# Selecting a chunk's blocks behind its ranks, a fetch at a late hand-out, a later gate for logits, and W1 halves in two even runs

## The chip, the cores and the metric

One core of one Trainium2 chip. The metric is the device time of one execution in microseconds (us): the median of three runs. A profiled execution beside them gives the time of every instruction. The engines: TensorE (PE, its weight loads PEld), VectorE (DVE), ScalarE (ACT), GpSimd (POOL) and the queue of SyncE (SP), which issues most of the transfers.

## The reference

A causal mixing step over seven tokens, then a mixture of experts with one expert a token:

```
x = conv(x, softmax(weight))           # 8 sequences x 3584 tokens x 192, 8 groups of 24 columns
logits = norm(x) @ norm(expert_emb).T / tau          # 28672 tokens, 8 experts
e = argmax(logits);  g = softmax(logits)[e]
out = g * (relu(x @ w1[e]) @ w2[e])    # w1[e]: 192 x 1024, w2[e]: 1024 x 192
```

## The kernel before

**Stages.** The tokens are cut into 16 chunks of 1792 (16 tiles of 112). For a chunk, `mix` computes the convolution on TensorE and the norms; `route` scales the rows, makes a two-part half-precision form of them, transposes it, computes the logits on TensorE, ranks each token within its expert, and leaves 16 scatters pending. Each scatter (POOL, line 959) writes 112 rows into a DRAM area sorted by expert, `rows_d`. Once 16 more scatters have been issued, and if the next chunk's number is in `PICK` (3, 4, 5, 6, 8, 10, 12, 14), `put` marks it and `settle` hands out new blocks: `hand_out` calls `pick`, which works out how many whole blocks of 1024, 512 or 256 tokens must exist whatever the routing was, and `select` computes on DVE, in 21 small instructions (17 without the update of the start positions), which expert and which first row each of them has. A block's expert is known only on the chip: SP and DVE load it from the tile `sel` into a register.

**A block.** `expert` works on up to 512 tokens. `fetch` issues on SP a transposing transfer of the block's rows from `rows_d` (line 1087) and of its gates and token numbers (line 1090), and names the scatters that it needs. DVE copies the expert's W1 (line 1069) and W2 (line 1072) into one `slot`. TensorE computes the hidden layer (`h_ps`, line 1142), ACT takes the relu as the first half-precision part (line 1146), DVE the rest as the second (line 1148), TensorE computes the output (`o_ps`, line 1170), ACT scales it and POOL sends it out (line 1177). Blocks are up to three ahead in fetching.

**W1 halves.** Behind a block of 128 tokens the next W1 is copied in two halves, each as soon as the hidden layer has done with the old half; behind other blocks in one piece. The last blocks (22 of 128 tokens among 512s and 256s) make most of the halves: 48 copies of a half in all.

**Order.** SP's queue keeps the order in which the program issues. The order on the other engines is arranged by the framework, under hints: `under` puts an instruction behind the last hidden part on DVE, `over` behind the last ACT step, `behind` behind the last matmul. The program is written by one Python loop in `run`: it writes the blocks' work, and between two pieces of a block as much work of `mix` and `route` as fits. These are generators: each yields how many us of DVE and ACT work it has written, and is continued when the slack of the block's pieces, times a rate, has paid for it (`steer` sets the rate from `COST`, the DVE and ACT work of a chunk). A yielded `_Gate` holds a generator until the planner's clock `clk` has passed a time: the logits of a group (4 tiles) wait for the time at which SP has issued the group's transposes plus `LAND_T`.

**The transposes on SP.** For chunks 3 to 15, `route` has a group's four row transposes done by SP (line 955). There are two buffers: the sets of groups 0 and 1 are written as their rows are ready, the sets of groups 2 and 3 right behind the logits of groups 0 and 1. After each group's logits the loads of parts of a later chunk's x (line 480) are written. A fetch is written at the start of a block, so a set of transposes stands before or behind it on SP by the planner's clock.

Of the kernel before, what the change touches and what calls it, by code (L numbers as in the profile page):

```python
# [17 lines left out]
ALU = mybir.AluOpType  # L18
# [12 lines left out]
NT = 16  # L31
CT = TP * NT
# [9 lines left out]
PICK = (2, 3, 4, 5, 6, 8, 10, 12, 14)  # L42
GX = 4
NACT = 3
OUT = 1.9, 1.6
COST = 17.4, 15.6
WAIT = 0.5, 0.5
COST_A, COST_B = 10.0, 26.5
LEAD = 16.0
# [2 lines left out]
KMAX = 32  # L52
MORE = 3
# [8 lines left out]
LATE = 1.0  # L62
PICKED = 5.0
ACTS = 8, 10, 16
LAND_X, LAND_T = 9.0, 4.5
TURN, FETCH, PIECE = 5.1, 2.1, 1.4
RANK_L, RANK_P = 2.0, 1.5
STEP1, STEP2, STEPC, STEPL = 1.08, 1.98, 0.65, 0.62
SPACE, EVICT, SAVED = 1.54, 0.6, 8.0
SIGNAL, MOVED = 0.15, 1.8  # L70
DONE = 2.6, 7.9
# [67 lines left out]
class _Moe:  # L139
    def __init__(self, ctx, tc, x, weight, emb, tau, w1, w2, out):  # L140
        self.tc, self.nc = tc, tc.nc
        self.x, self.weight, self.emb, self.tau = x, weight, emb, tau
        self.w1, self.w2, self.out = w1, w2, out
        B, S, _ = x.shape
        self.B, self.S, self.N = B, S, B * S
        self.nch = self.N // CT
        self.per_b = S // CT
        self.cap = self.N + PAD
        self.dummy = E * self.cap
        pool = lambda name, bufs, **k: ctx.enter_context(  # L150
            tc.tile_pool(name=name, bufs=bufs, **k))
        self.cp = pool("const", 1)
        self.xp = pool("xload", 2)
        self.xtp = pool("xtrans", 2)
        self.sp = pool("small", 2)
        self.lp = pool("lone", 1)
        self.ep = pool("expert", 3)
        self.fp = pool("flip", 2)
        self.yp = pool("y", 3)
        self.op = pool("out", 4)  # L160
        self.mp = pool("meta", 6)
        self.rings = {k: pool("ps_" + k, n, space=PSUM)
                      for k, n in (("r", 2), ("l", 1), ("h", 5))}

        self.res1 = self.cp.tile([128, E * IMG], F16, name="res1")
        self.res2 = self.cp.tile([128, E * IMG], F16, name="res2")
        self.slot = self.cp.tile([128, RES], F16, name="slot")
        self.rows = [self.cp.tile([TP, NT, RW], I32, name=f"rows{k}")
                     for k in range(2)]
        self.hid = self.cp.tile([128, 2 * NFC * 512], F16, name="hid")  # L170
        self.dp = pool("scratch", 1, space=DRAM)
        self.rows_d = self.dp.tile([E * self.cap + PAD, RW], I32, name="rows_d")
        self.scatters, self.pend, self.step = [], [], None
        self.drop = self.cp.tile([128, D], F16, name="drop")
        self.acc = self.cp.tile([128, 2 * E], F32, name="acc")
        self.counts, self.pace = {}, 1.0
        self.due_out, self.sent_at, self.next_out = 0.0, 0.0, None
        self.whole = None
        self.xts, self.mixed = [], {}
        self.clk, self.gated, self.mm = 0.0, False, None  # L180
        self.asked, self.sp_at, self.low, self.parts = {}, 0.0, None, []
        self.need = 0
        self.subs, self.ready, self.flips, self.at, self.copied = [], 0, 0, 0, 0


# [609 lines left out]
    def route(self, c):  # L795
        xTs = []
        nc, sp = self.nc, self.sp
        xc, s, si, f = self.mixed.pop(c)
        r32 = self.rows[c % 2]
        rows = r32[:].bitcast(F16)  # L800
        for g in range(0, NT, GX):
            u = slice(g, g + GX)
            sb = s[:, u].unsqueeze(2).to_broadcast([TP, GX, D])
            self.under(nc.vector.tensor_tensor(  # L804
                out=xc[:, u, :], in0=xc[:, u, :], in1=sb, op=ALU.mult).ins)
# [3 lines left out]
                out=rows[:, u, 256:384], in0=xc[:, u, 0:128],  # L809
                in1=rows[:, u, 0:128], op=ALU.subtract).ins)  # L810
            self.under(nc.vector.tensor_tensor(
                out=rows[:, u, 192:256], in0=xc[:, u, 128:192],
                in1=rows[:, u, 128:192], op=ALU.subtract).ins)
# [7 lines left out]
        for g in range(NT // GX):  # L821
            if c > DIRECT:
                if len(xTs) == g:
                    xTs.append((self.turn(rows, g * GX, GX), self.queue(TURN)))
                xT, at = xTs[g]
                yield _Gate(at + LAND_T)
            else:
                xT = self.xtp.tile([128, GX, 3, TP], F16, tag="xT", name="xT")
                for k in range(3):
                    tp = self.ps("r", [128, GX, TP], F16, "tr_ps")  # L830
                    for a in range(GX):
                        self.behind(nc.tensor.transpose(
                            out=tp[:, a, :],
                            in_=rows[:, g * GX + a, k * 128:(k + 1) * 128],
# [4 lines left out]
            for a in range(GX):  # L839
                for k in range(3):  # L840
                    i = nc.tensor.matmul(  # L841
                        out=lg[:, g * GX + a, :], lhsT=xT[:, a, k, :],
# [12 lines left out]
        if self.gated and self.step is not None:  # L855
# [4 lines left out]
            out=l, in_=lg.rearrange("p t (k e) -> p t e k", k=2), op=ALU.add,  # L860
# [14 lines left out]
                                op=ALU.mult)  # L875
        nc.vector.scalar_tensor_tensor(
            out=l, in0=l, scalar=0.0, op0=ALU.is_equal,
            in1=self.e8[:].unsqueeze(1).to_broadcast([TP, NT, E]), op1=ALU.mult)
# [4 lines left out]
                                op=ALU.is_equal)  # L883
# [5 lines left out]
            out=fl(inc[:]), data0=fl(self.rst[:]), data1=fl(oh[:]), initial=0.0,  # L889
# [12 lines left out]
            out=off, in0=pc[:TP, 0, :], in1=self.cb[:TP, :], op=ALU.add).ins)  # L902
        nc.vector.tensor_tensor(out=self.cb, in0=pc[:, 1, :], in1=self.cb,
                                op=ALU.add)
# [10 lines left out]
            out=di, in_=dr, scalar=-1.0, op=ALU.add)  # L915
        yield 0.8, 0.0
        self.pend += [(c, di[:, t:t + 1], r32[:, t, :]) for t in range(NT)]
        if c == self.nch - 1:
            self.pads()


    def put(self, step=None):
        if not self.pend:
            return
        c, idx, src = self.pend.pop(0)
        self.scatter(idx, src)
        if step is not None:
            _dep(self.tc, self.scatters[-1], step.name)
        if c < self.nch and len(self.scatters) % NT == 0:
            self.left += CT  # L930
            if c + 1 in PICK[1:]:
                self.whole = c + 1


    def settle(self):
        if self.whole is not None:
            self.hand_out(self.whole)
            self.whole = None


    def tick(self, us, i):
# [43 lines left out]
        self.pend += [(self.nch, p[:, e:e + 1], z) for e in range(E + 1)]  # L985


    def select(self, n, k, last, name, cb):
        nc, cp = self.nc, self.cp
        sh = n.bit_length() - 1  # L990
        one = lambda nm, shape=(1, E), dt=F32: self.lp.tile(
            list(shape), dt, tag="sl_" + nm, name="sl_" + nm)
        av, ai = one("av"), one("ai", dt=I32)
        nc.vector.tensor_tensor(out=av, in0=cb, in1=self.start,
                                op=ALU.subtract)
        nc.vector.tensor_single_scalar(out=ai, in_=av,
                                       scalar=float(n - 1 if last else 0),
                                       op=ALU.add)
# [45 lines left out]
                op0=ALU.mult, op1=ALU.add)  # L1044
        for j in range(k):
            for u in range(0, n, 512):
                self.subs.append((sel, j, n, u, self.need))


    def copy_w1(self, at, halves=(0, 1)):  # L1050
        nc = self.nc
        if at == len(self.subs) or self.subs[at][3]:
            return
        halves = [h for h in halves if self.copied <= 2 * at + h]
        if not halves:
            return
        if halves[0] == 0:
            sel, j = self.subs[at][:2]
            (i,), (self.we,) = nc.values_load_multi_w_load_instructions(
                sel[0:1, j, 0:1], engines=[nc.vector.engine], min_val=0,  # L1060
                max_val=(E - 1) * IMG,
                skip_runtime_bounds_check_because="select clamps it")
            self.under(i.ins)
        self.copied = 2 * at + halves[-1] + 1
        v = self.res1[:, bass.ds(self.we, W2)].rearrange(
            "p (k h f) -> p h k f", k=3, h=2)
        o = self.slot[:, 0:W2].rearrange("p (h k f) -> p h k f", k=3, h=2)
        h = slice(halves[0], halves[-1] + 1)
        self.under(nc.vector.tensor_copy(out=o[:, h], in_=v[:, h]).ins)  # L1069

    def copy_w2(self):
        self.nc.vector.tensor_copy(  # L1072
# [114 lines left out]
            yield OUT  # L1187


    def pick(self, n, last=False, most=KMAX):  # L1190
        k = (self.left + E * (n - 1)) // n if last else max(
            0, -((E * (n - 1) - self.left) // n))
        k = min(k, most)
        at = len(self.subs)
        if k:
            self.select(n, k, last, f"sel{n}_{self.left}", self.now)
            self.left -= k * n
        new = self.subs[at:]
        del self.subs[at:]
        w = max(1, n // 512)  # L1200
        return [new[i:i + w] for i in range(0, len(new), w)]
# [37 lines left out]
    def head(self, first):  # L1239
# [27 lines left out]

        def pick():
            self.left = first * CT
            self.hand_out(first)  # L1270

        def more():
            self.subs += sum(self.pick(128, most=MORE), [])

        n = p = P.add("DVE", 3.8, pick, ranked[-1], pri=PICKED)
        for _ in range(3):
# [6 lines left out]
        self.sp_at = 0.0  # L1283


    def hand_out(self, c):
        self.now, self.need = self.counts[c], NT * c
        for n in (1024, 512, 256) if c < 9 else (1024, 512):
            self.subs += sum(self.pick(n), [])
        self.end = ([p for p in PICK if p > c] + [self.nch])[0]  # L1290


# [14 lines left out]
        self.pace = (due - len(self.scatters)) / max(1.0, steps - MARGIN)  # L1307

    def last_blocks(self):
        self.now, self.need = self.cb[0:1, :], len(self.scatters)  # L1310
        big = self.pick(1024)
        mid = self.pick(512) + self.pick(256)
        small = self.pick(128, True)
        runs = [[((i + o) / (len(g) + o), b) for i, b in enumerate(g)]
                for g, o in ((big, 0.5), (mid, 0.5), (small, 3.0)) if g]
        for _, b in sorted(sum(runs, []), key=lambda v: v[0]):
            self.subs += b
# [69 lines left out]
```

## Time and profile before

| | us |
|---|---|
| median of 3 runs | 1247.41 (1246.84 to 1250.33) |
| the profiled execution | 1254.54 |
| its span, first to last instruction | 1252.8 |
| TensorE busy (matmul) | 1149.4 |
| DVE busy | 898.0 |
| ACT busy | 597.0 |
| POOL busy | 545.9 |

The mean granted clock of TensorE was 0.959 of full speed. Up to about 125 us the experts' weights are loaded and scaled and the first two chunks are routed; up to about 940 us chunks are routed beside the blocks; behind that there are blocks alone. A wait in a row is the idle time of an engine ahead of an instruction, with the instruction whose end released it.

### The profile page before, as it was taken

How to read it: one execution, taken by the hardware profiler on the slowest of the kernel's cores; microseconds unless marked ns; L12 is line 12 of the kernel's file. 1: busy time of each engine (PE TensorE's matmuls, PEld its weight loads, DVE VectorE, ACT ScalarE, POOL GpSimd, SP SyncE). 2: the span in 40 equal slices, each digit the busy share in tenths (PEclk: the TensorE clock that was granted, in tenths of full speed). 3: DMA queues.
4: the chain of work that ended last, by engine and by line, in shares of the span. 5: the costliest groups of instructions: out<-in, count | busy, mean ns of one | idle time of the engine just before them, and what ended most of it. 6: DMA issues, size and time to landing. Idle time of an engine off the chain costs nothing. (4 is left out here: it accounts for less than half of the span.)

```text
span 1252.8 us, 29845 instructions
## 1 busy us (share of the span) xinstructions
PE 1149.4 (92%) x10924; PEld 928.8 (74%) x10924; DVE 898.0 (72%) x2337; ACT 597.0 (48%) x1363; POOL 545.9 (44%) x541
## 2 busy tenths in 40 slices
PE   5637988899899899999899999999999999999997
PEld 3624877787878799678766666776677777889997
DVE  5996979688677878777576766756445566567786
ACT  5777835355253645556353645433433333333332
POOL 1271254564545565454545546455542221222222
PEclk9557999899899999999999999999999999999999
DMA  9851474563636465662736565363222112111211
GB/s 267 249 181 39 94 151 99 125 131 88 143 76 160 90 140 116 139 144 52 155 79 148 113 137 118 70 124 81 67 66 55 46 39 50 49 39 44 46 44 24
DMA packets 269187, 127.79 MB, mean 102 GB/s; under 512 B 210494, under 2 KB 259005, under 8 KB 269040
## 3 DMA queue, kind: packets, MB, share of 16 engines
q1 hardware_dynamic: 245216, 79.00, 29.5%
q0 software_dynamic: 23808, 46.87, 13.8%
q8 instruction: 86, 1.41, 0.5%
q14 instruction: 61, 0.50, 0.1%
q10 hardware_dynamic: 16, 0.01, 0.0%
HBM read 38.35 MB, written 47.53 MB: 69 GB/s over the span
## 5 line engine op out<-in xcount | busy, mean ns | idle before, releaser
L1142 PE MATMUL h_ps<-e_xT,slot 128*128 128x256 f16 (+2 forms) x3232 | 512.5, 291 | 27.8 <-DMA e_xT<-rows_d 18.4
L1170 PE MATMUL o_ps<-slot,hid 128*128 128x192 f16 x5544 | 494.5, 247 | 8.4 <-DVE hid L1148 5.1
L1142 PEld LDWEIGHTS <-slot 128*128 128x128 f16 x4040 | 354.5, 99 | 187.2 <-issue 31.0
L1170 PEld LDWEIGHTS <-hid 128*128 128x128 f16 x5544 | 461.2, 98 | 39.3 <-issue 11.6
L1177 POOL DMA_INDIRECT out_dram<-y,e_mt x231 | 254.3, 1101 | 471.3 <-ACT y L1175 428.4
L1148 DVE SCALAR_TENSOR_TENSOR hid<-h_ps,hid 128x512 f16<-128x512 f32 x462 | 312.7, 686 | 125.5 <-ACT hid L1146 122.9
L1146 ACT ACTIVATE hid<-h_ps 128x512 f16<-128x512 f32 x462 | 272.7, 597 | 233.9 <-PE h_ps L1142 229.0
L959 POOL DMA_INDIRECT rows_d<-rows,di x256 | 274.6, 1073 | 185.6 <-PE h_ps L1142 74.3
L1175 ACT ACTIVATE y<-o_ps,g 128x192 f32<-128x192 f32 x231 | 95.4, 419 | 320.0 <-PE o_ps L1170 294.9
L1142 PE MATMUL h_ps<-e_xf,slot 128*128 128x256 f16 (+2 forms) x808 | 220.4, 289 | 0.6 <-DVE e_xf L1109 0.4
L1072 DVE COPY slot<-res 128x3074 f16 x101 | 99.7, 987 | 139.7 <-PE o_ps L1170 139.1
L1069 DVE COPY slot<-res 128x3072 f16 (+1 forms) x125 | 118.8, 951 | 0.4
L759 PE MATMUL conv_ps<-xt,band 128*112 128x384 f32 x208 | 83.8, 495 | 1.2 <-ACT xt L764 1.2
L1109 DVE COPY e_xf<-e_xT 64x256 f16<-64x256 f16 (+2 forms) x202 | 47.2, 234 | 33.4 <-DMA e_xT<-rows_d 29.3
L764 ACT COPY xt<-conv_ps 112x384 f32<-112x384 f32 x104 | 49.4, 479 | 35.9 <-PE conv_ps L759 32.9
L841 PEld LDWEIGHTS <-xT 128*112 128x112 f16 x672 | 47.5, 132 | 20.9 <-DMA xT<-rows 13.9
L841 PE MATMUL lg_ps<-ma,xT 128*112 128x16 f16 x448 | 49.0, 193 | 11.5 <-DMA xT<-rows 10.8
L771 ACT ACTIVATE sq<-xt 112x192 f32<-112x192 f32 x156 | 55.7, 361 | 3.0 <-DVE sq L775 1.8
L806 ACT CAST rows<-xt 112x768 f16<-112x768 f32 x56 | 45.2, 833 | 16.7 <-DMA rows_d<-rows,di 5.6
L804 DVE TENSOR_TENSOR xt<-xt,x_p_s 112x768 f32<-112x768 f32 x56 | 50.7, 948 | 0.1
L808 DVE TENSOR_TENSOR rows<-xt,rows 112x512 f16<-112x512 f32 x56 | 38.3, 684 | 7.9 <-ACT rows L806 7.0
L841 PE MATMUL lg_ps<-mb,xT 128*112 128x16 f16 x224 | 39.2, 196 | 0.3 <-ACT xT L836 0.3
(211 smaller groups left out, 642.8 us busy)
## 6 DMA issues: line engine op xcount, KB each, us to landing
xt<-in_dram SPq DMA_DIRECT2D x42, 384.0 KB
res<-in_dram SPq DMA_DIRECT2D x6, 768.0 KB
rows_d<-rows,di POOLq DMA_INDIRECT x256
out_dram<-y,e_mt POOLq DMA_INDIRECT x231
xT<-rows SPq DMA_TRANSPOSE x208
res<-in_dram SPq DMA_DIRECT2D x6, 512.0 KB
xt<-in_dram SPq DMA_DIRECT2D x2, 1536.0 KB
xt<-in_dram SPq DMA_DIRECT2D x2, 1440.0 KB
```

The costliest lines, as they stand in the source:

```text
L759: i = nc.tensor.matmul(out=ps, lhsT=self.band[:, h, :], rhs=xt[:, :, h * G:(h + 1) * G], start=True, stop=True).ins
L771: self.over(nc.scalar.activation(out=sq, in_=xc[:, t, :], func=AF.Square, accum_out=n2[:, t:t + 1]).ins)
L841: i = nc.tensor.matmul(out=lg[:, g * GX + a, :], lhsT=xT[:, a, k, :], rhs=self.mb if k == 1 else self.ma, start=(k == 0), stop=(k == 2)).ins
L959: i = self.nc.gpsimd.indirect_dma_start(out=self.rows_d[:, :], out_offset=bass.IndirectOffsetOnAxis(ap=idx, axis=0), in_=src, in_offset=No ...
L1069: self.under(nc.vector.tensor_copy(out=o[:, h], in_=v[:, h]).ins)
L1072: self.nc.vector.tensor_copy(out=self.slot[:, W2:], in_=self.res2[:, bass.ds(self.we, IMG)])
L1142: self.mm = nc.tensor.matmul(out=ps[:, c, :], lhsT=w1(o, b + c), rhs=xk[k], start=(i == 0), stop=(i == 4)).ins
L1146: self.step = nc.scalar.activation(out=hh[:, b:b + m, :], in_=ps, func=AF.Relu).ins
L1148: self.low = nc.vector.scalar_tensor_tensor(out=hl[:, b:b + m, :], in0=ps, scalar=0.0, in1=hh[:, b:b + m, :], op0=ALU.max, op1=ALU.subtrac ...
L1170: self.mm = nc.tensor.matmul(out=o, lhsT=h[:, c, q], rhs=w2[:, c, k:k + D], start=(n == 0), stop=(n == 3 * NFC - 1)).ins
L1175: self.step = nc.scalar.activation(out=y, in_=o, func=AF.Copy, scale=g[:, a:a + 1]).ins
L1177: i = nc.gpsimd.indirect_dma_start(out=self.out[:, :], out_offset=bass.IndirectOffsetOnAxis(ap=mt[:, a, 0:1], axis=0), in_=y, in_offset=No ...
```

## The change

- Behind a chunk's ranks `route` itself calls `pick` for the next number of `PICK`, books 4.0 us of DVE work (`SELECT`) for each size that gave blocks, and keeps the blocks in `chosen`; `hand_out` takes them from there. The first instruction of `select` gets the hint `under`.
- `settle` fetches at once, up to two blocks ahead, if at a hand-out at most one block is left besides the new ones.
- `LAND_T` goes from 4.5 to 6.0, `COST` for DVE from 17.4 to 20.0.
- A copy of one W1 half is written as two runs of 256 columns of each of the three rows, the run's number outermost.

```diff
-COST = 17.4, 15.6
+COST = 20.0, 15.6
-LAND_X, LAND_T = 9.0, 4.5
+LAND_X, LAND_T = 9.0, 6.0
+SELECT = 4.0
...
         self.pend += [(c, di[:, t:t + 1], r32[:, t, :]) for t in range(NT)]
+        self.left += CT
         if c == self.nch - 1:
             self.pads()
+        elif c + 1 in PICK:
+            chosen = []
+            for n in self.sizes(c + 1):
+                at = self.left
+                chosen += sum(self.pick(n, c + 1), [])
+                if self.left < at:
+                    yield SELECT, 0.0
+            self.chosen[c + 1] = chosen
...
         if c < self.nch and len(self.scatters) % NT == 0:
-            self.left += CT
             if c + 1 in PICK[1:]:
                 self.whole = c + 1
     def settle(self):
-        if self.whole is not None:
+        if self.whole is not None and self.whole in self.chosen:
             self.hand_out(self.whole)
             self.whole = None
+            if len(self.subs) - self.at <= len(self.handed) + 1:
+                while self.ready < min(self.at + 2, len(self.subs)):
+                    self.fetch()
...
-        nc.vector.tensor_tensor(out=av, in0=cb, in1=self.start,
-                                op=ALU.subtract)
+        self.under(nc.vector.tensor_tensor(
+            out=av, in0=cb, in1=self.start, op=ALU.subtract).ins)
...
-        h = slice(halves[0], halves[-1] + 1)
-        self.under(nc.vector.tensor_copy(out=o[:, h], in_=v[:, h]).ins)
+        if len(halves) == 1:
+            o, v = (t[:, halves[0]].rearrange("p k (g f) -> p g k f", g=2)
+                    for t in (o, v))
+        self.under(nc.vector.tensor_copy(out=o, in_=v).ins)
...
+    def sizes(self, c):
+        return (1024, 512, 256) if c < 9 else (1024, 512)
     def hand_out(self, c):
-        self.now, self.need = self.counts[c], NT * c
-        for n in (1024, 512, 256) if c < 9 else (1024, 512):
-            self.subs += sum(self.pick(n), [])
+        self.handed = self.chosen.pop(c)
+        self.subs += self.handed
```

What is left out passes the counts and the number of needed scatters to `select` as arguments.

## Rows read from the trace of the kernel before

**Rows 1.** The page's first part (busy us, share of the span, instructions).

```profile
PE 1149.4 (92%) x10924; PEld 928.8 (74%) x10924; DVE 898.0 (72%) x2337; ACT 597.0 (48%) x1363; POOL 545.9 (44%) x541
```

**Rows 2.** Three of the page's forty slices: length, busy us (instructions) by engine, clock, DMA.

```profile
156.60:187.90 31.30, 26.49 (x279) 23.47 (x277) 21.97 (x86) 12.43 (x43) 18.63 (x20) 0.95 0.74 151
219.20:250.60 31.40, 27.75 (x254) 23.87 (x255) 20.89 (x54) 11.99 (x23) 15.98 (x16) 0.89 0.58 125
1190.20:1221.50 31.30, 30.92 (x383) 29.31 (x381) 25.25 (x44) 12.33 (x23) 8.08 (x7) 1.00 0.20 44
```

**Rows 3.** Who TensorE waited for: us in total, times, longest.

```profile
PE h_ps L1142 <- DMA e_xT<-rows_d: 18.4, 6, 4.5
PE lg_ps L841 <- DMA xT<-rows: 10.8, 18, 1.2
PE h_ps L1142 <- DVE slot L1069: 9.1, 13, 4.8
```

**Rows 4.** TensorE in time order (start, us, instructions, idle before): four waits.

```profile
177.20 2.08 PE L1142 MATMUL h_ps<-e_xT,slot 128*128 128x256 f16 x9 [3.93 <-DMA e_xT<-rows_d]
222.85 1.44 PE L1142 MATMUL h_ps<-e_xT,slot 128*128 128x256 f16 x6 [4.54 <-DMA e_xT<-rows_d]
346.83 0.90 PE L1142 MATMUL h_ps<-e_xT,slot 128*128 128x256 f16 x6 [3.71 <-DMA e_xT<-rows_d]
627.86 1.44 PE L1142 MATMUL h_ps<-e_xT,slot 128*128 128x256 f16 x6 [4.14 <-DMA e_xT<-rows_d]
```

**Rows 5.** SP's queue in time order ahead of the first of them.

```profile
166.11 5.07 SPq L955 DMA_TRANSPOSE xT<-rows  x4
172.61 1.29 SPq L1087 DMA_TRANSPOSE e_xT<-rows_d  x1
```

**Rows 6.** Copies on DVE by shape (count, busy us, mean ns, idle before).

```profile
L1069 DVE COPY slot<-res 128x3072 f16 x77 | 73.6, 956 | 0.4
L1069 DVE COPY slot<-res 128x1536 f16 x48 | 45.2, 941 | 0.0
L1109 DVE COPY e_xf<-e_xT 64x512 f16<-64x512 f16 x54 | 15.6, 289 | 1.1
```

**Rows 7.** Who the weight loads waited for from 950 us on.

```profile
PEld L1142 <- DVE slot L1069: 5.5, 13, 0.6
```

**Rows 8.** DVE in time order behind one block of 128 tokens.

```profile
1197.02 0.94 DVE L1069 COPY slot<-res 128x1536 f16 x1
1198.47 0.94 DVE L1069 COPY slot<-res 128x1536 f16 x1
1199.45 0.40 DVE L1109 COPY e_xf<-e_xT 64x128 f16<-64x128 f16 x2
```

**Rows 9.** The weight loads there.

```profile
1199.47 2.20 PEld L1142 LDWEIGHTS <-slot 128*128 128x128 f16 x36 [0.58 <-DVE slot L1069]
```

**Rows 10.** The clock behind two waits for row transposes (columns as in rows 2).

```profile
316.70:323.50 6.80, 6.21 (x44) 5.81 (x44) 3.80 (x14) 0.00 (x0) 1.13 (x1) 0.50 0.41 91
```

**Rows 11.** DVE behind chunk 2's ranks: counts, first and last of 21 instructions.

```profile
163.49 0.15 DVE L907 COPY cb<-cb 1x8 f32<-1x8 f32 x1
163.81 0.15 DVE L994 TENSOR_TENSOR sl_av<-cb,start 1x8 f32<-1x8 f32 x1
170.50 0.15 DVE L1042 SCALAR_TENSOR_TENSOR start<-sl_t,start 1x8 f32<-1x8 f32 x1
```

**Rows 12.** POOL's scatters: chunk 2's last, chunk 3's first, chunk 11's last.

```profile
198.66 1.07 POOL L959 DMA_INDIRECT rows_d<-rows,di  x1 [3.17 <-PE conv_ps L759]
211.21 0.94 POOL L959 DMA_INDIRECT rows_d<-rows,di  x1 [0.31 <-issue]
701.05 1.38 POOL L959 DMA_INDIRECT rows_d<-rows,di  x1 [2.63 <-PE h_ps L1142]
```

**Rows 13.** SP's queue at the hand-out near 701 us.

```profile
705.26 1.48 SPq L1087 DMA_TRANSPOSE e_xT<-rows_d  x1
```

**Rows 14.** TensorE at the first block of that hand-out.

```profile
715.49 1.03 PE L1142 MATMUL h_ps<-e_xT,slot 128*128 128x512 f16 x4
```

More of the change, by code (lines that the diff above doesn't have):

```diff
@@ L181, in __init__ @@
         self.asked, self.sp_at, self.low, self.parts = {}, 0.0, None, []
-        self.need = 0
+        self.chosen = {}
         self.subs, self.ready, self.flips, self.at, self.copied = [], 0, 0, 0, 0
@@ L985, in pads, with select @@
         self.pend += [(self.nch, p[:, e:e + 1], z) for e in range(E + 1)]
-    def select(self, n, k, last, name, cb):
+    def select(self, n, k, last, name, cb, need):
         nc, cp = self.nc, self.cp
@@ L1046, in select @@
             for u in range(0, n, 512):
-                self.subs.append((sel, j, n, u, self.need))
+                self.subs.append((sel, j, n, u, need))
     def copy_w1(self, at, halves=(0, 1)):
@@ L1187, in expert, with pick @@
             yield OUT
-    def pick(self, n, last=False, most=KMAX):
+    def pick(self, n, c=None, last=False, most=KMAX):
         k = (self.left + E * (n - 1)) // n if last else max(
@@ L1195, in pick @@
         if k:
-            self.select(n, k, last, f"sel{n}_{self.left}", self.now)
+            self.select(n, k, last, f"sel{n}_{self.left}",
+                        self.cb[0:1, :] if c is None else self.counts[c],
+                        len(self.scatters) if c is None else NT * c)
             self.left -= k * n
@@ L1269, in pick @@
             self.left = first * CT
+            self.chosen[first] = sum(
+                (sum(self.pick(n, first), []) for n in self.sizes(first)), [])
             self.hand_out(first)
         def more():
-            self.subs += sum(self.pick(128, most=MORE), [])
+            self.subs += sum(self.pick(128, first, most=MORE), [])
         n = p = P.add("DVE", 3.8, pick, ranked[-1], pri=PICKED)
@@ L1309, in last_blocks @@
     def last_blocks(self):
-        self.now, self.need = self.cb[0:1, :], len(self.scatters)
         big = self.pick(1024)
         mid = self.pick(512) + self.pick(256)
-        small = self.pick(128, True)
+        small = self.pick(128, last=True)
         runs = [[((i + o) / (len(g) + o), b) for i, b in enumerate(g)]
```

## The prediction

> **What bounds the kernel now.** I read first the page's busy shares and the row of granted clock, then the forty slices, then who waits for whom on TensorE and on SP's queue, and last the time order around the longest waits. The page gives TensorE as the engine with by far the most work, 92% of the span [rows 1]. So a microsecond counts only where TensorE stands idle or runs at its lower rate. The reader is to see two kinds of stretch. From 1127 us to the end TensorE is busy 31 us of every 31.3 at full clock: only small gaps are left to win there [rows 2]. From 157 to 658 us there are slices with 3 to 5 us of idleness, and in six of them the mean clock is 0.95 (four, the slice at 157 us is one) or 0.89 (two, the one at 219 us is one), so that a part of the slice ran at 1.2 instead of 2.4 GHz [rows 2]. The first 125 us hold larger losses still, but the change alters nothing there except which routine emits the first selection.
>
> Who ends TensorE's idleness: the fetch of a block's tokens (18.4 us, 6 times), the transposes that the logits need (10.8 us, 18 times, none over 1.2 us), the W1 copy (9.1 us) [rows 3]. Four fetch waits make nearly all of the first number: 3.93, 4.54, 3.71 and 4.14 us [rows 4]. SP's queue shows where they come from. Its order is written out and kept. At 172.61 us the fetch goes out right behind four transposes of a later chunk's rows (5.07 us) and an x load; it needs 172.61 to 177.20 = 4.6 us until TensorE starts [rows 4, 5]. The other three look alike.
>
> **The change part by part.** The sum is made against the profiled execution, 1254.54 us (span 1252.8 us and 1.7 us around it). It is 7.1 us above the median of 1247.41 us, so I take the difference from the median.
>
> *Halved W1 copies.* A half of 1536 elements takes 941 ns, a whole of 3072 takes 956 ns: the halves run at half the rate per element [rows 6]. In a half the destination is one run of 1536 and the source three rows of 512 with gaps; the new view makes both 2 x 3 x 256, as the whole copy's source is already 2 x 3 x 512. No row shows this form. Bounds: 941 ns (nothing gained), and on the line through the fast copies, 289 ns for 512 elements and 956 for 3072, 0.26 ns an element: 289 + 1024 x 0.26 = 556 ns [rows 6]. I take 556, since the whole copy is the nearest row: -0.385 us for each of 48. What of it counts is where TensorE waits for them. From 950 us on these are 13 waits, 5.5 us, the longest 0.6 [rows 7]. Each follows two halves with the hidden part between them (1197.02 and 1198.47 us), and weights load at 1199.47 after 0.58 us [rows 8, 9]. Two halves win 0.77 us, more than the longest wait. Next late is the copy of the swapped tokens behind them (0.40 us), so I keep back 0.5: **-5.0 us**, bounds 0 and -5.5.
>
> The Trainium skill's page "VectorE: DVE Perf Modes" (What auto-detection actually checks) lets a 16-bit copy run at four elements a cycle if the outermost counts of source and destination are both even or equal. If the half counts as three rows on both sides, it had that rate before and the edit gains nothing; the 941 ns beside 956 speak against that, and for a destination taken as one run of 1536 against three rows: that pair the rule refuses, and the new view's pair it allows.
>
> *Logits wait longer (LAND_T 4.5 to 6.0).* The planner puts a group's logits 1.5 us later among TensorE's instructions. All 18 waits are at most 1.2 us, so each would go. Where SP itself is late the transposes slide too, so I take two thirds: **-7.0 us**, bounds 0 and -10.8. Behind two of these waits the clock falls to half from 316.7 to 323.5 us, where TensorE had waited for nothing else: 6.8 x 0.5 = 3.4 us [rows 10]. I count about half of it: **-1.5 us**, bounds 0 and -3.4.
>
> *The same edit on SP.* The transposes of groups 2 and 3 are issued when the logits of groups 0 and 1 have been placed, since there are two buffers. Placed 1.5 us later, a set can fall behind a fetch that it now precedes. Each fetch of [rows 4] has such a set directly ahead, so one exchange brings it 5 us forward, more than the wait. All four are worth 16.3 us, and the clock of the slices that hold them or follow them 0.05 x 31.3 = 1.6 us three times (157, 345, 626 us) and 0.11 x 31.3 = 3.4 us once (219 us) [rows 2], 8.2 together: bound -24.5. The other bound is two new collisions of the same size, 2 x (4 + 2) = +12. The order is a question of which comes first on the planner's clock, and the trace does not tell by how much. I take a third: **-8.5 us**. The moved transposes themselves pass one fetch, 1.3 us, and the load of its token numbers, under 2 us together [rows 5].
>
> *Selection behind the ranks.* The instructions stay the same, 21 of about 0.15 us on DVE, 3.2 us a selection; nine fall in the loop [rows 11]. The trace says that they run there already: order on DVE is not the written one, and chunk 2's selection begins at 163.81, 0.32 us behind the start of the copy of the counts, and ends at 170.65, while the last scatter before its use is at 198.66 [rows 11, 12]. So nothing is gained by time. What is lost is that it no longer only fills gaps: written earlier, it can precede the hidden part that TensorE needs. Bounds: 0 (this one spread over 6.8 us among other work, and the next long wait of TensorE, at 173 us, was the fetch's [rows 4, 11]) and 9 x 3.2 = +29. I take **+2.0 us**, near that row. The last selections, for the blocks at the end, stay where they were. The raised COST pays for the 4.0 us that a selection is now booked with: 0, bounds -1 and +1.
>
> *Fetch at a late hand-out.* It acts only if at most one block besides the new ones is left. The candidate is the hand-out near 701 us: the last scatter starts at 701.05, the fetch at 705.26, the block's first matmul at 715.49 without a wait [rows 12, 13, 14]. It waits for the scatter's landing, not for its turn: 0; if that cover goes, rival (e) has the price.
>
> Sum: -5.0 - 7.0 - 1.5 - 8.5 + 2.0 = -20.0; 1247.4 - 20.0 = **1227.4 us**.
>
> **The rivals.** (a) *SP's order gets no better.* For it: four tight fetches in one order say that tightness is usual. Then without the -8.5: 1236. (b) *All four fetch waits go.* For it: each has the same set in front. Then -5.5 - 10.8 - 3.4 - 24.5 + 2 = -42: 1205. (c) *New collisions take the place of the old*, +12 instead of -8.5: 1248. For it: nothing but the planner's clock decides, and every gate moves. Against: sets spread wider apart collide less. (d) *The halves stay at 941 ns*, because the outer count of three decides: without the -5.0, 1232. That is what the skill page's rule gives for equal counts. (e) *Slower: ranks come later.* Group 2's transposes wait for group 0's logits, so a chunk's ranks come up to 2 x 1.5 = 3.0 us later. Ranks are on the chain already: after chunk 2's last scatter at 198.66 the next one starts at 211.21 [rows 12]. If nothing absorbs it over nine chunks, the hand-out at 701 us comes 27 us later. Its margin is 715.49 - 705.26 - 4.6 = 5.6 us, so TensorE stands 21 us and loses 2 in clock: 1247.4 - 13.5 + 2 + 23 = 1259. It decides from a slip of some 17 us (5.6 and the 11.5 gained). Against: it needs two thirds of the largest slip, and where logits waited, 0.6 us on the mean (10.8 / 18), that much of the 1.5 us is no slip.
>
> **How the numbers follow.** Chances: forecast 0.41, (a) 0.19, (b) 0.12, (c) 0.13, (d) 0.04, (e) 0.11. No change means within 0.3%, about what a measurement of this kernel can tell: 1243.7 to 1251.2 us. Forecast, (a), (b) and (d) lie below: 0.76. Of (c), 0.11 lies within and 0.02 above; with (e), slower is 0.13. The forecast's own bounds run from (b) to (c). The range 1205 to 1250 leaves out (e), what of (b) goes lower and what of (c) goes higher, under 2 in 10.
>
> **What would show it.** Halves of 0.55 us, and no wait for them behind 950 us; if they stay at 0.94, the first step is wrong. TensorE's wait for row transposes at 2 to 5 us instead of 10.8. Fetch waits at 8 to 12 us, and a fetch that stands ahead of a set of four transposes on SP where it stood behind; more than 18 means (a) or (c). No new row in which TensorE waits long for the hidden part while a selection runs; if there is one, the +2.0 was too small. A first matmul waiting at the hand-out near 700 us would show (e). The prediction is wrong as a whole if waits of TensorE from 125 to 950 us do not shrink.

## The result, and the profile after

The changed kernel takes 1200.26 us (median of 4 runs, 1198.68 to 1202.03), the kernel before beside it 1248.87 us (4 runs): a ratio of 0.961, 95% interval 0.958 to 0.964, 48.6 us faster. Forecast were 1227.4 us and a range from 1205. The direction was right, the size less than half of what came. The profiled execution after took 1202.03 us (span 1200.3), that of before 1254.54 (span 1252.8).

The page's busy line of the changed kernel, to be held against [rows 1]:

```profile
PE 1129.8 (94%) x10924; PEld 922.8 (77%) x10924; DVE 877.1 (73%) x2337; ACT 597.3 (50%) x1363; POOL 549.7 (46%) x541
```

The work is the same, instruction for instruction in number. Where the 52.5 us between the two spans lie is seen in windows cut at the W2 copy of the 64th block (near 950 us before, 903 us after). First the kernel before (length, busy us and count of PE, PEld, DVE, ACT, POOL, clock, DMA share, GB/s):

```profile
125.00:950.00 825.00, 783.04 (x7255) 626.28 (x7254) 598.13 (x1677) 398.40 (x971) 428.53 (x416) 0.98 0.50 111
950.00:1252.80 302.80, 293.72 (x3191) 248.48 (x3189) 202.02 (x346) 110.27 (x209) 74.99 (x70) 1.00 0.19 43
```

The same of the changed kernel, then two of its stretches where the slices of [rows 2] stood:

```profile
125.00:903.00 778.00, 766.58 (x7251) 619.37 (x7251) 590.83 (x1657) 398.39 (x971) 433.34 (x416) 1.00 0.54 117
903.00:1200.30 297.30, 291.39 (x3196) 249.63 (x3194) 189.01 (x367) 110.98 (x210) 74.14 (x71) 1.00 0.20 45
147.00:183.00 36.00, 36.00 (x366) 31.48 (x363) 31.50 (x111) 20.13 (x58) 17.29 (x16) 1.00 0.53 113
210.00:241.00 31.00, 29.61 (x336) 27.99 (x337) 22.40 (x72) 10.12 (x19) 22.27 (x20) 1.00 0.80 152
```

47.0 us (825 - 778) come from the middle, 5.5 from the tail, none from the first 125 us. In the middle TensorE idles 11.4 us instead of 42.0, 30.5 less, and is busy 16.5 us less; its clock is full throughout, where six slices had shown less. Who TensorE waits for from 125 to 950 us, to [rows 3]:

```profile
PE lg_ps L842 <- DMA xT<-rows: 3.8, 5, 1.5
PE o_ps L1184 <- DVE hid L1162: 3.5, 5, 1.7
PE h_ps L1156 <- DMA e_xT<-rows_d: 1.9, 2, 1.3
PE h_ps L1156 <- DVE slot L1083: 0.6, 1, 0.6
PE o_ps L1184 <- ACT hid L1160: 0.6, 2, 0.4
```

Fetches fall from 18.4 to 1.9 us, transposes from 10.8 to 3.8 (the same kernel on another chip, e9 below: 3.6 and 3.0). SP's queue shows the exchange, to [rows 5]: the fetch, at 172.61 us before, now goes out at 163.40, ahead of the set of four.

```profile
163.40 1.25 SPq L1101 DMA_TRANSPOSE e_xT<-rows_d  x1
...
166.75 6.37 SPq L967 DMA_TRANSPOSE xT<-rows  x4
```

The copies by shape, to [rows 6], and one block of 128 tokens in the tail, to [rows 8]: a half takes 550 ns, not 941, and behind 903 us no weight load waits for one any more.

```profile
L1083 DVE COPY slot<-res 128x3072 f16 x77 | 74.0, 960 | 0.4 <-issue 0.2
L1083 DVE COPY slot<-res 128x1536 f16 x48 | 26.4, 550 | 0.0
```

```profile
1146.38 0.55 DVE L1083 COPY slot<-res 128x1536 f16 x1
1147.50 0.55 DVE L1083 COPY slot<-res 128x1536 f16 x1
1148.08 0.39 DVE L1123 COPY e_xf<-e_xT 64x128 f16<-64x128 f16 x2
```

### The profile page after: what moved, and what is told of

Same layout as the page of the kernel before. It is cut to its first block, busy times and chain, and to the rows that moved or that the text cites. A ratio compares the mean times of both kernels' runs of the same rounds, so it can differ in the third digit from the quotient of the medians.

```text
span 1200.3 us, 29865 instructions
## 1 busy us (share of the span) xinstructions
PE 1129.8 (94%) x10924; PEld 922.8 (77%) x10924; DVE 877.1 (73%) x2337; ACT 597.3 (50%) x1363; POOL 549.7 (46%) x541
## 5 line engine op out<-in xcount | busy, mean ns | idle before, releaser
L1156 PE MATMUL h_ps<-e_xT,slot 128*128 128x256 f16 (+2 forms) x3232 | 503.5, 288 | 7.4 <-DVE slot L1083 5.5
L1184 PE MATMUL o_ps<-slot,hid 128*128 128x192 f16 x5544 | 488.8, 246 | 4.4 <-DVE hid L1162 3.5
L971 POOL DMA_INDIRECT rows_d<-rows,di x256 | 278.6, 1088 | 144.1 <-PE h_ps L1156 40.8
L1083 DVE COPY slot<-res 128x3072 f16 (+1 forms) x125 | 100.4, 803 | 0.4 <-issue 0.2
L807 ACT CAST rows<-xt 112x768 f16<-112x768 f32 x56 | 46.2, 833 | 15.9 <-DVE xt L805 8.0
L805 DVE TENSOR_TENSOR xt<-xt,x_p_s 112x768 f32<-112x768 f32 x56 | 51.7, 951 | 0.2
L842 PEld LDWEIGHTS <-xT 128*112 128x112 f16 x672 | 44.0, 131 | 9.2 <-DMA xT<-rows 4.4
L842 PE MATMUL lg_ps<-ma,xT 128*112 128x16 f16 x448 | 43.6, 193 | 3.9 <-DMA xT<-rows 3.8
```

Of the source, the lines that this page charges most:

```text
L842: i = nc.tensor.matmul(out=lg[:, g * GX + a, :], lhsT=xT[:, a, k, :], rhs=self.mb if k == 1 else self.ma, start=(k == 0), stop=(k == 2)).ins
L971: i = self.nc.gpsimd.indirect_dma_start(out=self.rows_d[:, :], out_offset=bass.IndirectOffsetOnAxis(ap=idx, axis=0), in_=src, in_offset=No ...
L1083: self.under(nc.vector.tensor_copy(out=o, in_=v).ins)
L1156: self.mm = nc.tensor.matmul(out=ps[:, c, :], lhsT=w1(o, b + c), rhs=xk[k], start=(i == 0), stop=(i == 4)).ins
L1184: self.mm = nc.tensor.matmul(out=o, lhsT=h[:, c, q], rhs=w2[:, c, k:k + D], start=(n == 0), stop=(n == 3 * NFC - 1)).ins
```

## The experiments

Each ratio is against the kernel before on the same chip. Fetch and logits are TensorE's waits for `e_xT` and for `xT` from 125 to 950 us; in the row of the kernel before they are from [rows 3]. Clock is half of TensorE's busy time behind 125 us in the stretches whose granted clock was 0.50, the us of work lost to it. The mean clock of a stretch counts idle time too, and most of what it shows as lost over the whole span lies in the first 125 us, where the kernels hardly differ (20 to 22 us by the same count).

| | ratio (95%) | us against before | fetch | logits | clock |
|---|---|---|---|---|---|
| before | | | 18.4 | 10.8 | 12.0 |
| e9, the changed kernel | 0.959 (0.957, 0.960) | -51.2 | 3.6 | 3.0 | 0 |
| e1, gate alone | 0.977 (0.974, 0.980) | -26.7 | 4.2 | 10.1 | 1.7 |
| e2, four exchanges | 0.992 (0.989, 0.996) | -8.8 | 7.1 | 14.1 | 9.5 |
| e3, selection alone | 0.984 (0.981, 0.987) | -17.7 | 7.2 | 11.9 | 5.0 |
| e4, halves alone | 0.996 (0.992, 0.999) | -4.4 | 18.7 | 12.5 | 11.7 |
| e10, no late fetch | 0.978 (0.976, 0.980) | -27.1 | 16.5 | 7.0 | 3.6 |
| e11, gate undone | 0.977 (0.975, 0.980) | -29.7 | 3.1 | 11.9 | 3.2 |
| e12, no booking | 0.974 (0.972, 0.975) | -32.5 | 5.9 | 7.7 | 6.3 |
| e13, selected late | 0.958 (0.956, 0.961) | -51.7 | 0.6 | 3.3 | 1.7 |
| e14, late fetch alone | 1.003 (1.001, 1.004) | +3.2 | 15.5 | 16.2 | 11.8 |
| e15, gate 7.0 | 0.962 (0.960, 0.964) | -47.2 | 3.8 | 2.5 | 5.1 |
| e16, COST 17.4 | 0.963 (0.960, 0.965) | -46.2 | 5.8 | 3.9 | 1.7 |
| e17, rule on SP | 0.986 (0.984, 0.988) | -18.0 | none | 10.7 | 3.4 |
| e18, rule, changed kernel | 0.978 (0.976, 0.979) | -27.6 | 12.4 | 6.2 | 9.6 |

**e1: the gate alone.**

```diff
-LAND_X, LAND_T = 9.0, 4.5
+LAND_X, LAND_T = 9.0, 6.0
```

> The kernel before with LAND_T 6.0 instead of 4.5 and nothing else. Theory T (place of the fetch on SP): each of the four long fetch waits came from a set of four row transposes directly ahead of the fetch; with later logits the sets of chunks 3 and 4 are written behind fetches 5 and 10, so the fetch waits fall from 18 us to under 6, the half-clock stretches behind them go, and the logits' waits go too: 20 to 35 us faster. Rival S (the selection's place and its booking make the gain): only the logits' waits go, 7 to 11 us faster, and the fetch waits stay at 15 us or more.

Measured: -26.7 us. TensorE's waits and SP's queue at the block of [rows 5]:

```profile
PE lg_ps L841 <- DMA xT<-rows: 10.1, 15, 1.5
PE h_ps L1142 <- DMA e_xT<-rows_d: 4.2, 5, 2.3
```

```profile
164.32 1.24 SPq L1087 DMA_TRANSPOSE e_xT<-rows_d  x1
...
167.43 6.14 SPq L955 DMA_TRANSPOSE xT<-rows  x4
```

The gate moved the fetch ahead of the set. Fetch waits fall by 14.2 us and the clock's loss by 10.3: together nearly the whole gain. Theory T missed one point: the logits' waits, at which the edit aims, stay (10.8 to 10.1).

**e2: the order on SP, at four places, in the kernel before.**

```diff
     def turn(self, rows, t, n):
+        if t >= 2 * GX and self.ready in EARLY and self.ready < len(self.subs):
+            self.fetch()              # EARLY = 5, 10, 21, 45
```

> The kernel before, but at four places (blocks 5, 10, 21 and 45) the fetch is issued on SP ahead of the set of four transposes that stood directly in front of it; gates, selection, copies as before. Theory T: the four waits of about 4 us and the clock behind them go, 16 to 25 us faster. Rival G (the long waits only show that SP and VectorE are late as a whole, the next one takes their place): less than 6 us faster, and the transposes that are now behind the fetch make TensorE's logits wait 4 us or more longer in total.

Measured: -8.8 us (by the interval 5 to 14), less than T said and more than G. The exchanged fetches wait no more, but the next one (block 11) now stands behind two sets and is waited for. SP's queue, TensorE there, and its waits:

```profile
207.99 6.66 SPq L958 DMA_TRANSPOSE xT<-rows  x4
...
215.39 5.10 SPq L958 DMA_TRANSPOSE xT<-rows  x4
...
222.47 1.34 SPq L1090 DMA_TRANSPOSE e_xT<-rows_d  x1
```

```profile
228.70 0.98 PE L1145 MATMUL h_ps<-e_xT,slot 128*128 128x256 f16 x4 [3.46 <-DMA e_xT<-rows_d]
```

```profile
PE lg_ps L842 <- DMA xT<-rows: 14.1, 22, 1.4
PE h_ps L1145 <- DMA e_xT<-rows_d: 7.1, 3, 3.5
PE o_ps L1173 <- ACT hid L1149: 6.4, 3, 2.7
```

**e3: the selection part alone,** with its booking and COST 20.0. Of the change's hunks it has all but these:

```diff
+LAND_X, LAND_T = 9.0, 6.0
...
+            if len(self.subs) - self.at <= len(self.handed) + 1:
+                while self.ready < min(self.at + 2, len(self.subs)):
+                    self.fetch()
...
+            o, v = (t[:, halves[0]].rearrange("p k (g f) -> p g k f", g=2)
```

> The kernel before with the selection part alone: blocks are selected behind the ranks, 4.0 us booked for each size, COST 20.0; LAND_T stays 4.5, the halves stay as they were, no fetch at a late hand-out. Theory T: the booking delays the next chunk's rows on the planner's clock, so that fetches 5, 10 and 21 stand ahead of the sets of transposes as well: fetch waits under 8 us, 15 to 25 us faster although the logits' waits stay near 11 us. Rival L (only the longer gate LAND_T brings the gain): no faster than before by more than 3 us, or slower by some us for selections ahead of the hidden part.

Measured: -17.7 us, with fetch waits of 7.2, as T said. The prediction had priced this part at +2.0; it is a second, separate way to move fetches. The four waits of [rows 4] are gone here too; the longest that is left (2.86 us, at 477 us) is a new one.

**e4: the halves alone.**

```diff
-        h = slice(halves[0], halves[-1] + 1)
-        self.under(nc.vector.tensor_copy(out=o[:, h], in_=v[:, h]).ins)
+        if len(halves) == 1:
+            o, v = (t[:, halves[0]].rearrange("p k (g f) -> p g k f", g=2)
+                    for t in (o, v))
+        self.under(nc.vector.tensor_copy(out=o, in_=v).ins)
```

> The kernel before with the new view of the W1 halves alone. Half copies fall from 941 to about 550 ns. Theory T: this counts only behind 950 us, 4 to 7 us faster, and the waits from 125 to 950 us stay. Rival D (VectorE's load in the middle is what the gain came from): 10 us or more faster, with shorter waits before 950 us.

Measured: -4.4 us; 549 ns a half, and the middle's waits stay (fetch 18.7). Theory T. The three parts alone sum to 26.7 + 17.7 + 4.4 = 48.8 us, and the whole change gave 48.6. That the sum fits is chance: the same three parts together, without the late fetch, won 27.1 us (e10 below).

**e5 to e8** ran on a chip on which every kernel is slower (before: 1282.62 us), so they are compared with each other and with before only there. e5, e6 and e8 are the changed kernel with one part undone; e7 is the kernel before with LAND_T 6.0, the new halves, COST 20.0 and the booking alone.

```diff
-LAND_X, LAND_T = 9.0, 6.0           # e5
+LAND_X, LAND_T = 9.0, 4.5
-COST = 20.0, 15.6                   # e6
-SELECT = 4.0
+COST = 17.4, 15.6
+SELECT = 0.0
+        elif c + 1 in PICK:         # e7, in route behind the ranks
+            for _ in range(BOOK[c + 1]):    # 2 for 8, else 1
+                yield SELECT, 0.0
-            if len(self.subs) - self.at <= len(self.handed) + 1:    # e8
-                while self.ready < min(self.at + 2, len(self.subs)):
-                    self.fetch()
```

> The changed kernel with LAND_T back at 4.5. Theory P (the gate and the booking both act through the planner's clock, and what each gave alone, 26.7 and 17.7 us, adds up): 22 us faster than before, so about 1228 us, with fetch waits near 7 us and logits' waits of 10 us or more again. Rival O (with the booking in place the longer gate is no longer needed for the order on SP): within 6 us of the changed kernel, 1206 us or less.

> The changed kernel with SELECT 0.0 and COST 17.4: blocks are selected behind the ranks, but no time is booked for it. Theory P (the booking is what the selection part gave): as the longer gate and the halves alone, 26.7 + 4.4 = 31 us faster than before, about 1219 us, with logits' waits near 10 us. Rival S (the place of the selection in the program gave it): within 5 us of the changed kernel, 1205 us or less.

> The kernel before with LAND_T 6.0, the new halves, COST 20.0 and 4.0 us booked behind a chunk's ranks for each size that gives blocks, but blocks are still selected at the hand-out. Theory P: 43 to 50 us faster than before, about 1200 to 1207 us, with fetch waits under 4 us. Rival S: about 31 us faster, 1219 us, as without the selection part.

> The changed kernel without the fetch at a late hand-out. Theory P: as the changed kernel within 4 us, 1196 to 1204 us. Rival N (the fetch that goes out at once takes away a wait at hand-outs): 6 us or more slower than the changed kernel, with a fetch wait of 3 us or more behind one of the hand-outs.

Measured: 1270.48 (ratio 0.988), 1266.40 (0.986), 1288.80 (1.006) and 1286.91 us (1.002). e7 and e8 differ in where the blocks are selected, and in nothing else of the order written for SP: 1.9 us apart. Both, and of the four only they, have a fetch wait of 15.8 us, as rival N said of e8. That e7 would win 43 us or more was wrong: I had taken the late fetch to be worth nothing. The waits of e8 from 125 to 950 us:

```profile
PE o_ps L1181 <- issue: 21.9, 32, 2.6
PE h_ps L1153 <- DMA e_xT<-rows_d: 16.4, 2, 15.8
```

**e9 to e12: the changed kernel, and three parts taken out of it, side by side** (the edits of e8, e5 and e6).

> The changed kernel itself, as the anchor for the three kernels beside it on this chip (the chip of the four runs before this one was slower for every kernel: 1283 instead of 1250 us for the kernel before, with many waits of TensorE for nothing but its own instruction stream). Every theory: 0.96 of the kernel before if the chip is like the first one, between 0.96 and 0.985 if it is like the second.

> The changed kernel without the fetch at a late hand-out, beside the changed kernel. Theory N (booking delays the ranks, one hand-out near 700 us comes too late, and the fetch that goes out at once hides it): one fetch wait of about 16 us behind that hand-out and some 17 us at half clock, so 20 to 28 us slower than the changed kernel. Theory P (it acts on nothing here): within 4 us of the changed kernel; the long wait was the slow chip's.

> The changed kernel with LAND_T 4.5, beside the changed kernel. Theory P (gains add up): 20 to 28 us slower than the changed kernel; fetch waits near 7, logits' waits 10 us or more. Rival O (the booking alone settles the order on SP): under 8 us slower.

> The changed kernel with SELECT 0.0 and COST 17.4, beside the changed kernel. Theory P (the booking is the selection part's gain): 13 to 20 us slower than the changed kernel, logits' waits near 10 us. Rival S (the place of the selection is): within 5 us of it.

Measured: 1201.01 us; without the late fetch +24.1, without the gate +21.5, without the booking +18.7 (1225.14, 1222.47, 1219.68). In size theories N and P hold. In e10 TensorE stands 15.55 us at one hand-out. The granted clock is 0.50 for 17.1 us, but 13.0 of these are the wait itself; 4.1 us of work run at half clock, 2.0 us lost. Fetch waits make 12.9 and the clock 3.6 of e10's 24.1 us, longer waits of the logits 4.0. TensorE, SP's queue, the clock (in all, in the wait, behind it):

```profile
694.30 3.15 PE L1153 MATMUL h_ps<-e_xT,slot 128*128 128x512 f16 x7 [15.55 <-DMA e_xT<-rows_d]
```

```profile
672.14 10.31 SPq L964 DMA_TRANSPOSE xT<-rows  x8
...
683.26 5.34 SPq L964 DMA_TRANSPOSE xT<-rows  x4
...
690.25 1.69 SPq L1098 DMA_TRANSPOSE e_xT<-rows_d  x1
```

```profile
681.30:698.40 17.10, 4.10 (x10) 1.50 (x11) 1.94 (x8) 0.00 (x0) 2.64 (x4) 0.50 0.68 149
681.30:694.30 13.00, 0.00 (x0) 0.03 (x1) 1.24 (x6) 0.00 (x0) 1.97 (x3) 0.50 0.65 152
694.30:698.40 4.10, 4.10 (x10) 1.48 (x11) 0.70 (x3) 0.00 (x0) 0.67 (x1) 0.51 0.79 138
```

The same place in the changed kernel: the fetch passes the third set and is 11 us ahead of its block, whose first matmul at 673.52 us waits for nothing.

```profile
649.25 11.64 SPq L967 DMA_TRANSPOSE xT<-rows  x8
662.51 1.47 SPq L1101 DMA_TRANSPOSE e_xT<-rows_d  x1
...
666.15 2.24 SPq L1101 DMA_TRANSPOSE e_xT<-rows_d  x1
669.12 5.94 SPq L967 DMA_TRANSPOSE xT<-rows  x4
```

The booking does likewise. In e12 block 9's fetch stands behind a set of eight and is waited for; in the changed kernel the next chunk begins later on the planner's clock, and it stands ahead of that set. SP and TensorE in e12:

```profile
197.05 11.06 SPq L967 DMA_TRANSPOSE xT<-rows  x8
...
210.04 1.22 SPq L1101 DMA_TRANSPOSE e_xT<-rows_d  x1
```

```profile
214.21 0.58 PE L1156 MATMUL h_ps<-e_xT,slot 128*128 128x128 f16 x4 [3.43 <-DMA e_xT<-rows_d]
```

SP in the changed kernel:

```profile
190.06 1.21 SPq L1101 DMA_TRANSPOSE e_xT<-rows_d  x1
...
193.01 12.81 SPq L967 DMA_TRANSPOSE xT<-rows  x8
```

P's reason for e11 fails, though: the fetch waits do not come back without the gate (3.1 us against 3.6 in e9). With the booking in place the gate acts on the logits, whose waits rise from 3.0 to 11.9 us, and a little on the clock (3.2 us) and on the hidden part from ACT (0.4 to 2.8). e11's waits:

```profile
PE lg_ps L842 <- DMA xT<-rows: 11.9, 13, 2.0
PE h_ps L1156 <- DMA e_xT<-rows_d: 3.1, 3, 1.6
PE o_ps L1184 <- ACT hid L1160: 2.8, 2, 2.7
```

**e13 to e16.** e13 is e7 with the late fetch directly behind the selection at the hand-out; e14 has the late fetch alone in the kernel before; e15 and e16 are the changed kernel with another constant.

```diff
             self.hand_out(self.whole)       # e13 and e14
             self.whole = None
+            if len(self.subs) - self.at <= len(self.handed) + 1:
+                while self.ready < min(self.at + 2, len(self.subs)):
+                    self.fetch()
-LAND_X, LAND_T = 9.0, 6.0           # e15
+LAND_X, LAND_T = 9.0, 7.0
-COST = 20.0, 15.6                   # e16
+COST = 17.4, 15.6
```

> The changed kernel in all but one point: blocks are selected at the hand-out as before, while the 4.0 us are still booked behind the ranks and the fetch at a late hand-out goes out directly behind the selection. Theory P (the booking counts, not the place): within 4 us of the changed kernel, 1197 to 1206 us. Rival S (the early place is what lets the fetch go out at once): at the hand-out near 650 us SP waits for the selection, TensorE stands 3 us or more for a fetch, 1208 us or more.

> The kernel before with the fetch at a late hand-out alone. Theory P (it pays only where gate and booking together push a hand-out behind the last known block): within 4 us of the kernel before. Rival N (hand-outs are late in the kernel before as well): 6 us or more faster.

> The changed kernel with LAND_T 7.0. Theory P (once the fetches stand ahead of the sets and the clock is full, only some 7 us of idleness are left from 125 to 950 us): between 4 us faster and 4 us slower than the changed kernel. Rival G (every later gate wins a like amount, 22 us per 1.5 us): 10 us or more faster. Rival H (hand-outs get later): 8 us or more slower, with a long fetch wait near 650 us.

> The changed kernel with COST back at 17.4 for VectorE, the 4.0 us still booked. The planner then works off the chunks more slowly than they cost. Theory P (COST only pays for the booking): hand-outs come later, 5 to 25 us slower than the changed kernel, the loss in waits for fetches or chunks after 600 us. Rival: within 3 us of it, the rate is at its limit nearly everywhere.

Measured: 1199.45, 1254.37, 1204.00 and 1205.02 us beside 1251.17 for the kernel before. e13 has the changed kernel's ratio within both intervals: the place of the selection plays no part. What the selection part won it won by the planner's numbers, the booking and COST (e12). e14: the late fetch alone wins nothing (3.2 us slower, in its interval 0.8 to 5.5). e15: a later gate wins nothing more. e16 lies 4.8 us above the changed kernel by the ratios (1252 x 0.0038), just under what I expected, and 5.6 above e13 on its own chip; from e16 to e12, where the booking goes too, it is 14 us more (1252 x 0.0112). COST is the small part, the booking the large one.

**e17 and e18: a rule on SP.** A set written behind the end of a block's hidden layer lets the next fetch pass. e17 has it, and the late fetch, in the kernel before; e18 in the changed kernel.

```diff
     def turn(self, rows, t, n):
+        if self.gated and self.done:      # set at the end of a block's hidden layer
+            while self.ready < min(self.at + 3, len(self.subs)):
+                self.fetch()
```

> The kernel before with a rule: when a set of row transposes is written behind the end of a block's hidden layer, the next block's fetch is written ahead of it; and the fetch at a late hand-out. LAND_T 4.5, no booking, old halves. Theory U (the order on SP is the cause): fetch waits under 6 us instead of 18, 22 to 36 us faster. Rival V (gate and booking gain in other ways too, and transposes pushed back by a fetch make the logits wait): as at the four places, 6 to 15 us faster, logits' waits 14 us or more.

> The changed kernel with the same rule. Theory U: fetch waits there are 2 to 4 us already, so within 4 us of the changed kernel. Rival V: transposes pushed back by a fetch make the logits wait, 5 us or more slower.

Measured: -18.0 us in e17, between the two theories; e18's ratio is 0.019 above the changed kernel's, some 24 us slower, which refutes U there. e17's waits:

```profile
PE lg_ps L842 <- DMA xT<-rows: 10.7, 16, 1.6
PE h_ps L1150 <- DVE slot L1076: 5.5, 3, 2.6
PE o_ps L1179 <- DVE hid L1156: 5.0, 8, 2.2
```

The fetch waits are gone without gate or booking, and 8.6 us of the clock's loss: the order on SP gives that much (the late fetch, in e17 too, won nothing alone in e14). The logits' waits stay, and those for the W1 copy grow from 1.4 to 5.5 us, so it is not the whole gain. In e18 new collisions came (fetch waits 12.4 us, the longest 4.8, and 9.6 us lost to the clock): fetching earlier is no gain in itself. That the pushed sets caused them by moving the planner's later steps is likely, but not shown.

## Why the prediction was wrong

*The failed step is the order on SP.* "I take a third: -8.5 us", of a bound of -24.5. The gate alone (e1) took 14.2 us of fetch waits and 10.3 us of clock, together as much as that bound; the whole change took 16.5 of the 18.4 us and, with full clock everywhere from 125 us on, 12.0 us of clock. The mechanism was the one described, its size was three times the one taken (28.5 us, against 8.5 and the 1.5 of clock counted with the logits). Its clock terms were a little high, since a mean clock counts idle time too: by busy time the four places lose 7.2 us, not 8.2, and the stretch of [rows 10] 3.1, not 3.4. I took a third because the trace does not tell which comes first on the planner's clock. But the planner and its constants are in the code. By its clock the next block begins, with its fetch, 10.2 us after group 0's set is written; the logits' gate, which lets group 2's set out, opens after TURN + LAND_T = 5.1 + 4.5 = 9.6 us in the kernel before and 5.1 + 6.0 = 11.1 us with the edit. That is an exchange at the first of the four places, and one can know it by following the code. That the other three look alike was half right: ahead of the last two SP had two sets of four, as here before the wait at 346.83 us.

```profile
326.65 5.78 SPq L955 DMA_TRANSPOSE xT<-rows  x4
...
333.16 5.06 SPq L955 DMA_TRANSPOSE xT<-rows  x4
...
340.12 2.17 SPq L1087 DMA_TRANSPOSE e_xT<-rows_d  x1
```

Still none of the four long waits is left in e1 or in e3, so rival (b), given 0.12, was nearer to what came than a third. Nor was the gate the only way: in the changed kernel the booking alone would have settled the order (e11).

*"The raised COST pays for the 4.0 us that a selection is now booked with: 0".* The second failure. The booked time is no work, but it holds the next chunk back by some planner time, and with it sets that stood ahead of fetches: -17.7 us alone (e3), 18.7 lost without it and its COST (e12). The whole part was priced at +2.0 for instructions that cost nothing where they stand (e13).

*The late fetch, "0".* Right for the kernel before (e14), wrong for the changed one: with gate and booking the ranks come later, as rival (e) said, and one hand-out falls behind the last known block. Rival (e) priced that at 21 us of idleness and 2 of clock; e10 has 15.55 and 2.0. I had not put the two together: this hunk removes just that cost.

*Logits wait longer, -7.0 and -1.5.* The total is right (10.8 to 3.8 us), the cause not, so this agreement is luck: the gate alone leaves 10.1 (e1), the booking alone 11.9 (e3), and only both bring it to 3 (e9). Why it takes both is not settled. The half clock behind two of these waits did go with the gate alone (e1), though the waits stayed.

*Halves, -5.0.* Right: 550 ns where 556 were forecast, -4.4 us alone, -5.5 in the tail's window. The even pair of views runs at the rate of the whole copy, (956 - 550) / 1536 = 0.26 ns for each further element, which agrees with the rule of the Trainium skill's page "VectorE: DVE Perf Modes" (What auto-detection actually checks) that the prediction weighed.

*What is left.* Fetch waits 16.5, logits 7.0, waits for the hidden part from VectorE and ACT 4.0 (8.1 to 4.1): 27.5 of the 30.5 us of idleness in the middle. The clock is 12.0 of the 16.5 us of busy time there, the halves 5.5 in the tail: 45.0 of the 52.5 us between the spans. The other 3.0 us of idleness and 4.5 us of busy time I did not follow.

## What to carry to other kernels

In a queue that keeps its written order, a transfer behind a batch of others pays for the whole batch: look there first when an engine waits for a DMA, and ask of every edit to a planner's due times, costs or bookings which transfer changes places with which. Such an edit acts by thresholds: price it as all or nothing at each place, after following the planner's clock through the code, and price the parts of one change together, since one may be there to pay for another's side effect. Moving fetches ahead at chosen places or by a fixed rule brought new collisions with it: e2 kept 8.8 us of a bound of 24.5, and e18 lost 24. And where a stretch at half clock holds a wait, only half of the work in it is lost time; the rest is the wait, counted already.

## What the runs showed of the hardware

What a wait of TensorE costs in clock did not grow with the wait. At the four of [rows 4] (16.3 us) it worked 14.4 us at a granted clock of 0.50, 7.2 us lost, 1.4 to 2.6 each; at the one of 15.55 us it worked 4.1 us so, 2.0 lost. In the changed kernel, with no wait over 1.7 us from 125 us on, the clock never fell before the end; but in e13, with none longer either, it fell once (3.4 us near 336 us), so that is no rule. And chips differ: of five, four gave 1249 to 1252 us for the kernel before, one 1282.62, and its traces have waits of TensorE ahead of which nothing shown was late (21.9 us in 32 pieces in e8). On it the gate-undone and no-booking versions won 12 and 16 us, where they won 30 and 33 on another.
